# First chunk's q projection token tile by token tile, with weights in contiguous blocks of 128 channels

## The chip, the cores and the metric

One core of a Trainium2 chip runs the whole program. The metric is device time in microseconds (us) of one execution; lower is better. PE is TensorE's matmul side, PEld its weight loads, DVE is VectorE, ACT is ScalarE, SP is the engine whose queue issues nearly all DMAs. A hole is time on PE beyond the usual spacing between the starts of two matmuls. An evacuation copies a result out of PSUM, where this kernel's matmuls put it, into SBUF, where they read it.

A ratio is the mean time of one kernel's runs over that of the kernel before in the same rounds, so it is not quite the ratio of the medians quoted beside it.

## The reference, cut to what matters

Two layers, each an attention block with a residual and a gated feed-forward block with a residual, on 2,048 tokens of 1,024 channels in bf16:

```python
x = A_x                                              # [1, 2048, 1024]
x = x + _A_ref(_layernorm(x), A_wqkv, A_wo)          # q,k,v projections, 8 dilated keys per query, output projection
x = x + _B_ref(_layernorm(x), B_w1, B_w3, B_w2)      # silu(x w1) * (x w3), times w2
x = x + _A_ref(_layernorm(x), A_wqkv, A_wo)
x = x + _B_ref(_layernorm(x), B_w1, B_w3, B_w2)
```

Only the first thing that TensorE can do matters here: layernorm of the first 512 tokens ("chunk 0", four row tiles of 128 tokens) and their q projection with `A_wqkv[:, 0:1024]`.

## The kernel before

Tokens go in chunks of `CH = 512`. A chunk's normalized tokens are transposed into `xnT` (channel on the partition, token along the row). For q, k and v in turn, `q_part` multiplies 8 channel blocks of 128 by 8 contraction slices. The q, k, v projections of all four chunks come first, then attention (on DVE) and the feed-forward stages interleave.

The start of the kernel before normalizes all four row tiles, then projects:

```python
def ln_first(key):
    # ... stats on DVE for tiles 0..2, by two ACT accumulations for tile 3 ...
    warm(NWARM)                     # 13 dummy matmuls of 512 columns
    # stats, sqrt, apply and PE transposes of the 4 tiles, with 4 + 4 + 2 more dummy matmuls between them
    # evacuation of the transposes into xnT on ACT and DVE

def q_part(l, c, which, ws, then=()):
    first = (l, c) == (0, 0) and which < 2
    # ...
    for t0 in range(0, KT, SG):                         # SG = 2
        sgt = stg.tile([P, SG, CH], BF16, name="sgt")   # 3 staging buffers
        for t in range(t0, t0 + SG):
            ps = bank("ps")
            for kk in range(KT):
                nc.tensor.matmul(ps[:], lhsT=ws[kk // KH][:, kk % KH, t::KT], rhs=xnT[:, kk, :],
                                 start=(kk == 0), stop=(kk == KT - 1))
            # ...
            nc.scalar.copy(sgt[:, t - t0, :], ps[:])
            if first:                                   # attention's first q and k tile, directly
                nc.scalar.copy(now_T[:, t, HALO if which else 0:], ps[:, 0:TCH])
        nc.sync.dma_start(qkv_d[l][which][:, t0:t0 + SG, c * CH:(c + 1) * CH], sgt[:])
        # ... then[t0 // SG](): a later load
```

The weights are read with a step of 8 channels (`t::KT`), so that head channels land on the partitions that attention wants. Loads: x tiles 0, 1, 2 on SP and 3 on ACT's queue, then the q weights in four pieces of 512 KB, the k weights, x chunk 1. The loads of x chunk 2, both v weight tiles and x chunk 3 are issued one by one behind the four stores of q (`then`).

The order of work in the program is fixed when it is built, from a small cost model in the kernel (`now`, `x_at`): it decides after which projection step an output projection (`o_tile`, PE) of an attention half is placed:

```python
while o_queue and (must or oT_at.get((o_queue[0][0], o_queue[0][1] // 2), 1e9) + 0.3 <= now["pe"]):
    o_tile()
```

## Time and profile before

| | kernel before |
|---|---|
| time, median (range) | 1619.57 us (1619.52 to 1619.87, 6 runs) |
| span of the profiled run | 1617.9 us |
| first q matmul | 12.20 us |
| end of q (64 matmuls, 0.216 us apart) | about 26.0 us |
| q weight pieces landed (the trace's DMA records) | 8.19, 9.53, 10.87, 12.23 us |
| attention's first multiply on DVE | 45.86 us |

The page of the kernel before, its part on the chain that ended last (followed back from the last instruction, at each step to what released it; shares of the span by engine, then by line):

```profile
PE 98%; DVE 1%; issue 1%; DMA 0%; ACT 0%; SPq 0%; DVEq 0%
PE acc L609 24%; PE pu L593 23%; PE pg L585 23%; PE ps L543 20%; PE po L501 7%; DVE tm L432 0%; DMA x_sb<-in_A_x_dram 0%; DVE tm L317 0%; DVE hT L597 0%; DVE st L246 0%; DVE At L416 0%; DVE xn L259 0%; ACT xnT L277 0%; DVE xnT L277 0%; PE pT L269 0%
```

TensorE is the chain. The list of waits of PE alone, in the whole span (engine, line, what it waited for, us in total, times, longest):

```profile
PE pw L173 <- DVE hT L166: 1.2, 1, 1.2
PE pT L269 <- DVE xn L259: 0.6, 1, 0.6
PE ps L543 <- DVE xnT L277: 0.3, 1, 0.3
```

All three lie in the first 12.2 us. From the first q matmul on, PE starts a 512-column matmul every 0.216 us, to the last few. So the time is a prologue, a fixed amount of PE work, and a tail.

The timeline of the kernel before, a few lines of the prologue (start us, duration us, engine, line, operation, tiles, count, and in brackets the idle time before and who ended it):

```profile
1.19 5.51 PE L173 MATMUL pw<-hT 128*128 128x512 bf16 x13 [1.19 <-DVE hT L166]
...
6.61 0.62 PE L269 MATMUL pT<-ident,xn 128*128 128x128 bf16 x8
...
11.36 1.09 DVE L277 COPY xnT<-pT 128x1024 bf16<-128x1024 bf16 x3 [0.16 <-PE pT L269]
12.17 19.85 PEld L543 LDWEIGHTS <-wqkv 128*128 128x128 bf16 x93 [0.47 <-issue]
12.20 20.05 PE L543 MATMUL ps<-xnT,wqkv 128*128 128x512 bf16 x90 [0.33 <-DVE xnT L277]
```

The 13 dummy matmuls (5.51 us) start 0.427 us apart, where 512-column matmuls later start 0.216 us apart; that is what "half clock" means below. (The trace's granted clock says 1.00 there too; the spacing is what shows it.) The transposes of tile 0 follow at 6.61, and useful work starts at 12.20, released by an evacuation into `xnT` on DVE. Further on one hand-over is tight. The timeline of the kernel before again, at the output projection of the second attention half (`oT` is attention's result, L501 reads it):

```profile
160.19 0.29 DVE L319 TENSOR_TENSOR oT<-tm 128x256 bf16<-128x256 bf16 x1
160.51 3.34 PEld L501 LDWEIGHTS <-oT 128*128 128x128 bf16 x16
```

The first weight load of the projection starts at 160.51. The eight pieces of `oT` are read one after the other, 0.216 us apart, so the last one is needed at about 160.51 + 7 x 0.216 = 162.0; it is finished at 160.19 + 0.29 = 160.48.

### The profile page before, as it was taken

The numbers are of one execution on the slowest core, as the hardware profiler recorded it, in microseconds if no ns is written. First come the engines' busy times: TensorE is split into PE (matmuls) and PEld (weight loads), VectorE is DVE, ScalarE is ACT, GpSimd is POOL, SyncE is SP. The second block draws the span as 40 slices with busy tenths as digits, with TensorE's granted clock in tenths as the row PEclk, the third lists the DMA queues.
The fourth block names the chain that finished last, engine by engine and source line by source line (L and its number), as shares of the span: only waits on it lengthen the run. The fifth ranks groups of instructions, "written<-read, shape, count | busy, mean of one in ns | idle before, by whom it ended". The sixth has DMA issues, their size and how long they took to land.

```text
span 1617.9 us, 18887 instructions
## 1 busy us (share of the span) xinstructions
PE 1604.7 (99%) x7342; PEld 802.1 (50%) x7491; DVE 1176.1 (73%) x1962; ACT 358.8 (22%) x558; POOL 1.9 (0%) x12
## 2 busy tenths in 40 slices
PE   9999999999999999999999999999999999999999
PEld 5666544444445544455444554445544444444444
DVE  5999898989899899998998449983499832222222
ACT  5333311212112230222302123021230212011110
POOL 0000000000000000000000000000000000000000
PEclk9999999999999999999999999999999999999999
DMA  9465755466537664578553676538674265436430
GB/s 317 133 180 168 244 182 161 137 190 196 169 106 235 222 194 131 171 208 249 158 182 120 213 241 170 187 101 255 213 223 157 92 195 170 143 108 217 157 130 27
DMA packets 335322, 285.28 MB, mean 176 GB/s; under 512 B 69632, under 2 KB 317824, under 8 KB 335104
## 3 DMA queue, kind: packets, MB, share of 16 engines
q1 hardware_dynamic: 334944, 283.67, 57.7%
q8 instruction: 58, 0.95, 0.2%
q10 hardware_dynamic: 288, 0.39, 0.1%
q14 instruction: 32, 0.26, 0.0%
HBM read 238.94 MB, written 29.36 MB: 166 GB/s over the span
## 4 chain that ended last, share of the span: by engine, by line
PE 98%; DVE 1%; issue 1%; DMA 0%; ACT 0%; SPq 0%; DVEq 0%
PE acc L609 24%; PE pu L593 23%; PE pg L585 23%; PE ps L543 20%; PE po L501 7%; DVE tm L432 0%; DMA x_sb<-in_A_x_dram 0%; DVE tm L317 0%; DVE hT L597 0%; DVE st L246 0%; DVE At L416 0%; DVE xn L259 0%; ACT xnT L277 0%; DVE xnT L277 0%; PE pT L269 0%
## 5 line engine op out<-in xcount | busy, mean ns | idle before, releaser
L593 PE MATMUL pu<-xnT,w3t 128*128 128x512 bf16 x1760 | 420.8, 379 | 2.1
L585 PE MATMUL pg<-xnT,w1t 128*128 128x512 bf16 x1751 | 419.2, 379 | 1.8
L609 PE MATMUL acc<-w2t,hT 128*128 128x512 bf16 (+1 forms) x1769 | 387.7, 378 | 1.8
L543 PE MATMUL ps<-xnT,wqkv 128*128 128x512 bf16 x1506 | 331.3, 379 | 1.9 <-DVE xnT L277 0.3
L589 ACT ACTIVATE sg<-pg 128x512 bf16<-128x512 f32 x224 | 133.6, 597 | 767.5 <-PE pg L585 709.4
L597 DVE TENSOR_TENSOR hT<-sg,pu 128x512 bf16<-128x512 bf16 x224 | 152.8, 682 | 185.3 <-PE pu L593 173.7
L609 PEld LDWEIGHTS <-hT 128*128 128x128 bf16 x1804 | 176.6, 98 | 210.5
L593 PEld LDWEIGHTS <-w3t 128*128 128x128 bf16 x1792 | 175.4, 98 | 211.4
L585 PEld LDWEIGHTS <-w1t 128*128 128x128 bf16 x1792 | 175.3, 98 | 211.4
L543 PEld LDWEIGHTS <-wqkv 128*128 128x128 bf16 x1536 | 220.3, 143 | 111.9 <-issue 0.5
L372 DVE TENSOR_TENSOR pr<-qT,kT 128x2048 bf16<-128x2048 bf16 x128 | 156.4, 1222 | 88.5 <-DMA kT<-qkv_d 86.4
L547 ACT CAST sgt<-ps 128x512 bf16<-128x512 f32 x192 | 111.9, 585 | 243.1 <-PE ps L543 218.0
L619 DVE TENSOR_TENSOR x_sb<-x_sb,acc 128x512 bf16<-128x512 bf16 x129 | 87.4, 677 | 107.5 <-PE acc L609 102.8
L432 DVE TENSOR_TENSOR tm<-At,vT 128x2048 bf16<-128x2048 bf16 x128 | 156.3, 1221 | 2.4
L317 DVE TENSOR_TENSOR tm<-tm 128x1024 bf16<-128x1024 bf16 (+1 forms) x256 | 134.7, 552 | 0.4
L317 DVE TENSOR_TENSOR pr<-pr 128x1024 bf16<-128x1024 bf16 (+1 forms) x256 | 134.5, 553 | 0.5
L501 PE MATMUL po<-wo,oT 128*128 128x512 bf16 x501 | 115.2, 379 | 0.6
L192 DVE BATCH_NORM_STATS2 st<-x_sb 128x6 f32<-128x512 bf16 x120 | 75.9, 672 | 8.8 <-DMA x_sb<-in_A_x_dram 8.8
L501 PEld LDWEIGHTS <-oT 128*128 128x128 bf16 x512 | 50.1, 98 | 60.0
L506 DVE TENSOR_TENSOR x_sb<-x_sb,po 128x512 bf16<-128x512 bf16 x64 | 43.4, 685 | 20.9 <-PE po L501 20.6
L589 ACT ACT_TABLE_LOAD x31 | 39.8, 1283 | 50.5 <-PE pg L585 46.2
L319 DVE TENSOR_TENSOR psm<-pr 128x256 bf16<-128x256 bf16 x128 | 36.7, 287 | 0.5
(88 smaller groups left out, 377.1 us busy)
## 6 DMA issues: line engine op xcount, KB each, us to landing
w1t<-in_B_w_dram SPq DMA_DIRECT2D x56, 1024.0 KB, 5.6
w3t<-in_B_w_dram SPq DMA_DIRECT2D x56, 1024.0 KB, 8.0
w2t<-in_B_w_dram SPq DMA_DIRECT2D x48, 1024.0 KB, 5.3
wqkv<-in_A_wqkv_dram SPq DMA_DIRECT2D x28, 1024.0 KB, 6.9
qkv_d<-sgt SPq DMA_DIRECT2D x96, 256.0 KB, 3.1
w2t<-in_B_w_dram SPq DMA_DIRECT2D x16, 512.0 KB, 5.1
qT<-qkv_d SPq DMA_DIRECT2D x15, 512.0 KB, 9.1
kT<-qkv_d SPq DMA_DIRECT2D x14, 544.0 KB, 9.2
```

The lines of the kernel that those rows point to most:

```text
L317: nc.vector.tensor_tensor(b[:, 0:m, :], b[:, 0:m, :], b[:, m:2 * m, :], op=ALU.add)
L372: V.tensor_tensor(pr[:], qT[:], kT[:, :, k0:k0 + TCH], op=ALU.mult)
L432: V.tensor_tensor(tm[:], At[:], win, op=ALU.mult)
L501: nc.tensor.matmul(ps[:], lhsT=oT[:, t, j * P:(j + 1) * P], rhs=wo[:, t, hh * 512:(hh + 1) * 512], start=(t == 0), stop=(t == KT - 1))
L543: nc.tensor.matmul(ps[:], lhsT=ws[kk // KH][:, kk % KH, t::KT], rhs=xnT[:, kk, :], start=(kk == 0), stop=(kk == KT - 1))
L547: nc.scalar.copy(sgt[:, t - t0, :], ps[:])
L585: nc.tensor.matmul(pg[:], lhsT=w1t[:, kk, fi * P:(fi + 1) * P], rhs=xnT[:, kk, :], start=(kk == 0), stop=(kk == KT - 1))
L589: nc.scalar.activation(sg[:], pg[:], ACTF.Silu)
L593: nc.tensor.matmul(pu[:], lhsT=w3t[:, kk, fi * P:(fi + 1) * P], rhs=xnT[:, kk, :], start=(kk == 0), stop=(kk == KT - 1))
L597: nc.vector.tensor_tensor(hT[:, f - f0, :], sg[:], pu[:], op=ALU.mult)
L609: nc.tensor.matmul(acc[:], lhsT=hT[:, f - f0, j * P:(j + 1) * P], rhs=w2ts[(f - f0) // 8][:, (f - f0) % 8, q0:q0 + step], start=(f == f0), ...
L619: nc.vector.tensor_tensor(xs, xs, acc[:], op=ALU.add)
```

## The change

The intent is to start useful matmuls right after the first row tile's norm (near 7 us) instead of after the fourth's (12.2 us). With 128 tokens in hand a matmul has 128 columns, so the weights should load fast; they are now read in contiguous blocks of 128 channels, and the store to DRAM puts channels back where attention expects them. Attention's first q tile is then loaded from DRAM rather than copied from PSUM. Weights come in slices of 256 KB, interleaved with the x tiles. The dummy matmuls between transposes are gone.

```diff
-    def ln_first(key):                       # all four norms, then q_part(0, 0, 0)
+    def first_q(ws, loads, then):
+        q_rows = qkv_d[0][0][:].rearrange("i t s -> (i t) s").rearrange("(b p) s -> p b s", p=P)
+        load_tile(0, 0, 512, nc.sync)
+        load_tile(0, 512, D, nc.scalar)
+        load_tile(1, 0, D, nc.sync)
+        loads(0, 2)                          # weight slices 0, 1
+        load_tile(2, 0, D, nc.sync)
+        loads(2, 4)
+        load_tile(3, 0, D, nc.sync)
+        loads(4, 8)                          # then k weights, x chunk 1
         ...
+        def product(out, kk, b, tok, start, stop):
+            nc.tensor.matmul(out, lhsT=ws[kk // KH][:, kk % KH, b * P:(b + 1) * P], rhs=xnT[:, kk, tok], ...)
         ...                                  # norm, transpose, evacuation of tile 0
+        for kk in range(6):                  # tile 0, 128 columns, one weight slice after the other
+            step0(kk)
+        stats(2, 0)
+        xn = apply(1)
+        pTs = transpose(xn)
+        for h in range(2):
+            evacuate(1, h, pTs, nc.scalar.copy)
+        for kk in range(6, KT):
+            step0(kk)
+        stats(2, 1)
+        deviation(2)
         ...
+        stats(3, 0)
+        xn = apply(2)
+        stats(3, 1)
+        deviation(3)
+        for b in range(3):                   # tile 1, 128 columns; transposes of tiles 2 and 3 in between
+            block1(b)
         ...
+        tok = slice(2 * P, CH)               # tiles 2 and 3 together, 256 columns
+        for i, acc in enumerate(accumulators(2, 2 * P)):
             ...
+            nc.scalar.copy(hT[:, 2 * i:2 * i + 2, tok], acc[:])
+            nc.sync.dma_start(q_rows[:, 2 * i:2 * i + 2, 0:CH], hT[:, 2 * i:2 * i + 2, :])
+            then[i]()                        # x chunk 2, v weights, x chunk 3
@@ q_part (now k of chunk 0 first)
+            if first and t0 == SG:
+                load_part(qT, 0, 0, 0, False)    # attention's first q tile, from DRAM
@@ planner
-    now = dict(pe=12.5, dve=12.5, act=12.5, table=None)
-    x_at = [12.5, 22.0, 27.0, 36.0]
+    now = dict(pe=22.0, dve=15.0, act=22.0, table=None)
+    x_at = [12.5, 20.0, 25.0, 34.0]
```

The planner's start values are changed along with the rest.

## The prediction

> **What bounds it now.** TensorE. The page gives PE 99% busy and 98% of the chain of work that ended last. Reading PE's instructions in order of time, the matmuls of 512 columns start 0.216 us apart from 12.2 us to 1614.5 us, with no hole above 20 ns that isn't a missing record. So the time is about 12.2 us of prologue, some 7,424 matmuls at 0.216, and a 3 us tail. Only the stretch up to the end of the first q projection (64 matmuls, 12.2 to about 26.0 us) changes.
>
> **The prologue now.** Timeline: 13 cold warm-up matmuls 0.427 us apart until 6.6 us; first transposes at 6.6; last norm evacuation near 12.4; first q matmul at 12.2. The DMA issues of the trace land the q weights at 8.2, 9.5, 10.9 and 12.2 us; the windows show 356 to 397 GB/s from 5 us on. So norm and weights finish together: starting tile by tile helps only as far as weights are there.
>
> **Cost of the new order.** 128-column products: the transposes in the timeline (8 in 0.62 us, the last end modelled 0.22 us long) start 56 ns apart, each with its own weight load. The Trainium skill, "TensorE: Matmul & The Clock Gate", Back-to-back issue gap, gives 55.6 ns alone, but about 81 ns sustained for load-and-matmul streams; I follow the trace. Two tiles are 2 x 64 x 56 ns = 7.2 us, the 256-column rest 64 x 0.109 = 7.0 us, transposes of tiles 1 to 3 1.35 us: 15.5 us against 13.8 + 0.
>
> Bytes are unchanged (1 MB x, 2 MB weights before k), so I estimate w5 at about 10.7 us and w7 at about 12.1. Tile 0 therefore crawls at weight speed (0.67 us a slice, 0.45 us of work) and ends at 12.6. Then ACT is the brake: evacuation of tile 1 in two copies (0.58 us each, between the 0.37 and 1.0 us seen for 256 and 1024 elements), the square roots of tiles 2 and 3 behind it in its order. I expect holes of about 0.5 us before tile 1 and 0.5 us before tile 3's transposes. q then ends at 12.6 + 3.6 + 0.9 + 7.0 + 1.0 = about 25.0, against 26.0. DMA a bit earlier would give 24.
>
> **Downstream.** All of that 1 to 2 us lies on PE's chain, since PE never waits later. Against it: the loads of x chunks 2 and 3 hang on the later q stores (first store near 20.5 us against 16.5), so attention on VectorE starts no earlier (45.9 us now). The second attention half ends at 160.5 us and its output projection starts at 160.7: an earlier PE may wait there and give back up to 1 us, unless the planner moves that tile one step later.
>
> **Predicted: 1618.4 us, range 1616.6 to 1619.9.** Faster by over 2%: 0.01; within 2%: 0.98; slower: 0.01.
>
> **Right if:** first q matmul at about 7.5 us; 128-column matmuls 56 ns apart; tile 0's steps released by weight DMAs; q's last matmul at 24 to 25.5 us; k, v and all later work spaced 0.216, shifted by a constant.
>
> **Wrong if:** q ends by 22 to 23 (weights land earlier than I estimate: about 1616); 128-column pairs take 80 ns (q ends 3 us later: about 1621); the clock gate drops to half because the PE is only about 65% busy from 7 to 12 us and the filler matmuls are gone (same page, HAM: an idle window of about 3.4 us throttles; here 107 ns spacing would show it, costing 1 to 2 us); or a wait of the first output projections for attention returns the gain.

## More of the kernel before

Staging buffers (`sgt`) hold results until a DMA has stored them.

Runs of one submission share a chip and share the runs of the kernel before.

## The result, and the profile after

| | before | after |
|---|---|---|
| time, median (range), 6 runs each | 1619.57 us (1619.52 to 1619.87) | 1618.28 us (1617.55 to 1619.09) |
| span of the profiled run | 1617.9 us | 1616.3 us |
| first q matmul | 12.20 us | 7.35 us |
| end of q (start of k) | about 26.0 us | 24.64 us |
| last q weights landed | 12.23 us | 12.22 us |
| PE's last matmul starts | 1614.50 us | 1613.09 us |
| attention's first multiply | 45.86 us | 47.74 us |

The ratio is 0.9992, with an interval of 0.9979 to 1.0005. In all rounds, though, the slowest of the changed kernel's 11 timed runs (1619.22 us) is faster than the fastest of the kernel before's (1619.40 us): a gain of about 1 us is there. Also new is the scatter: a range of 1.5 us against 0.35.

The page after, chain that ended last:

```profile
PE 99%; DMA 0%; SPq 0%; DVE 0%; ACT 0%; issue 0%
PE acc L658 24%; PE pu L642 24%; PE pg L634 24%; PE ps L591 20%; PE po L552 7%; PE pq L283 1%; DMA wqkv<-in_A_wqkv_dram 0%; SPq L683 0%; SPq L241 0%; DVE xn L266 0%; ACT xnT L280 0%; PE pT L275 0%; DVE st L255 0%; ACT sd L259 0%; DVE x_sb L668 0%
```

The q weights (`DMA wqkv<-in_A_wqkv_dram`) now stand on the chain, in place of the norm. PE's instructions after, in order of time:

```profile
6.28 0.72 PE L275 MATMUL pT<-ident,xn 128*128 128x128 bf16 x8
7.35 2.19 PE L283 MATMUL pq<-xnT,wqkv 128*128 128x128 bf16 x32 [0.35 <-ACT xnT L280]
10.25 1.30 PE L283 MATMUL pq<-xnT,wqkv 128*128 128x128 bf16 x16 [0.70 <-DVE st L255]
11.38 0.61 PE L275 MATMUL pT<-ident,xn 128*128 128x128 bf16 x8
11.83 2.40 PE L283 MATMUL pq<-xnT,wqkv 128*128 128x128 bf16 x40
14.06 0.61 PE L275 MATMUL pT<-ident,xn 128*128 128x128 bf16 x8
14.51 1.06 PE L283 MATMUL pq<-xnT,wqkv 128*128 128x128 bf16 x16
15.86 0.62 PE L275 MATMUL pT<-ident,xn 128*128 128x128 bf16 x8 [0.29 <-DVE xn L266]
16.32 8.49 PE L283 MATMUL pq<-xnT,wqkv 128*128 128x128 bf16 x88
24.64 1.67 PE L591 MATMUL ps<-xnT,wqkv 128*128 128x512 bf16 x7
```

Read single, the 128-column products start 56 ns apart and the 256-column ones 109 ns apart. The first 24 run without a break, the weight slices 0 to 2 having landed; slices 3, 4 and 5 each give a burst of 8 that had to wait for its slice. The trace's DMA records land the eight slices at 5.98, 6.63, 7.99, 8.88, 10.20, 10.88, 11.54 and 12.22 us; the hole that ends at 10.25 is thus slice 4. (The view puts it down to `DVE st`, whose instruction happened to end at 10.25 too. PE reads nothing of it; the weight load just before, at 10.24, waited 0.87 us for `DMA wqkv`, and in the run `wlate` below the hole itself is put down to the DMA.) Behind slice 7 there is one hole, 0.45 us before 15.86, where tile 3's norm comes late. The chain that ended last, in order of time, ties both together:

```profile
5.11 5.77 DMA wqkv<-in_A_wqkv_dram
10.88 0.05 issue
10.93 0.62 PE pq L283 x8
...
15.86 0.62 PE pT L275 x8
```

The last landing on it is slice 5's (10.88). Behind its 8 products PE transposes tile 1, ACT evacuates it (from 11.81), and only then comes tile 2's square root in ACT's order (12.88), and tile 3's norm after that (14.73 to 15.81). Slices 6 and 7 aren't on this chain, but slice 7 is a near tie: PE's work from slice 5's first product (10.93) to slice 7's (12.28) takes 1.35 us, the landings of the two are 1.34 us apart. So a distance counted from slice 7, as in the table below, serves as well as one counted from slice 5.

Behind q, PE has no hole over 20 ns in this run. From k's first matmul to PE's last one it takes 1588.45 us, as before (about 1588.5, with q's end worked out as 12.20 + 64 x 0.216). That distance will be used below: what it exceeds 1588.45 by is PE time lost behind q.

The slack at the output projection of the second attention half is now gone. The timeline after:

```profile
159.11 1.39 PEld L552 LDWEIGHTS <-oT 128*128 128x128 bf16 x7
...
160.38 0.29 DVE L371 TENSOR_TENSOR oT<-tm 128x256 bf16<-128x256 bf16 x1
160.73 1.71 PEld L552 LDWEIGHTS <-oT 128*128 128x128 bf16 x9 [0.23 <-DVE oT L371]
```

PE came 1.4 us earlier, attention 0.2 us later, which uses up the 1.5 us. The eighth weight load of the tile now waits for the last piece of `oT`, 0.23 us, which the matmuls in flight just cover.

Why attention didn't come earlier too: the timeline after, among k's results:

```profile
39.76 0.59 ACT L595 CAST sgt<-ps 128x512 bf16<-128x512 f32 x1 [3.48 <-DMA qkv_d<-sgt]
...
40.51 0.31 ACT L194 ACTIVATE sd<-mv,epst 128x2 f32<-128x2 f32 x1
...
40.85 0.17 DVE L201 RECIPROCAL rstd<-sd 128x2 f32<-128x2 f32 x1 [2.29 <-ACT sd L194]
```

ACT stands 3.48 us for a staging buffer (`sgt`) whose store sits in the SP queue behind later loads and DMA transposes. A norm's square root is next in ACT's order, DVE waits 2.29 us for it, and attention is next in DVE's order.

### The profile page after: what moved, and what is told of

It reads as the page before. It is cut to its first block, busy times and chain, and to the rows that moved or that the text cites. A ratio compares the mean times of both kernels' runs of the same rounds, so it can differ in the third digit from the quotient of the medians. Undisturbed runs are those within 1.5% of the kernel's fastest.

```text
span 1616.3 us, 19263 instructions
## 1 busy us (share of the span) xinstructions
PE 1610.7 (100%) x7609; PEld 805.3 (50%) x7609; DVE 1176.6 (73%) x1965; ACT 353.6 (22%) x547; POOL 1.9 (0%) x12
## 4 chain that ended last, share of the span: by engine, by line
PE 99%; DMA 0%; SPq 0%; DVE 0%; ACT 0%; issue 0%
PE acc L658 24%; PE pu L642 24%; PE pg L634 24%; PE ps L591 20%; PE po L552 7%; PE pq L283 1%; DMA wqkv<-in_A_wqkv_dram 0%; SPq L683 0%; SPq L241 0%; DVE xn L266 0%; ACT xnT L280 0%; PE pT L275 0%; DVE st L255 0%; ACT sd L259 0%; DVE x_sb L668 0%
## 5 line engine op out<-in xcount | busy, mean ns | idle before, releaser
L591 PE MATMUL ps<-xnT,wqkv 128*128 128x512 bf16 x1472 | 319.2, 379 | 0.0
L591 PEld LDWEIGHTS <-wqkv 128*128 128x128 bf16 x1472 | 211.1, 143 | 106.7
L595 ACT CAST sgt<-ps 128x512 bf16<-128x512 f32 x184 | 106.7, 585 | 230.7 <-PE ps L591 211.9
L446 DVE STREAM_TRANSPOSE psmT<-psm 128x2048 bf16<-128x2048 bf16 x16 | 36.9, 2306 | 0.2
```

## The experiments

All kernels gave correct results. Where a run's edit is said to be on top of another, it has that one's edit too. The table gives what the profiled run of each shows. "Slice 7" is the landing of the last q weights, "q end" the start of k's first matmul, "lost" the PE time lost behind q as defined above, "attention" the start of its first multiply. Every time is in us; the last column is the kernel before.

| run | slice 7 | q end | q end minus slice 7 | lost | attention | median (range) | before |
|---|---|---|---|---|---|---|---|
| after (result) | 12.22 | 24.64 | 12.42 | 0.00 | 47.74 | 1618.28 (1617.55 to 1619.09) | 1619.57 |
| again | 11.82 | 24.24 | 12.42 | 0.89 | 48.30 | 1618.72 (1618.48 to 1619.22) | 1619.61 |
| wlate | 12.56 | 24.98 | 12.42 | 0.87 | 48.99 | 1619.73 (1619.00 to 1620.16) | 1619.61 |
| norms | 12.49 | 24.45 | 11.96 | 1.09 | 48.71 | 1618.49 (1618.02 to 1619.02) | 1619.61 |
| strided | 12.10 | 24.78 | 12.68 | 1.02 | 48.96 | 1618.58 (1618.53 to 1619.29) | 1619.61 |
| loads | 11.88 | 24.30 | 12.42 | 0.01 | 45.82 | 1618.11 (1617.42 to 1618.55) | 1619.64 |
| dual | 12.18 | 23.41 | 11.23 | 0.45 | 47.02 | 1617.86 (1617.34 to 1618.19) | 1619.64 |
| dual_loads | 12.35 | 23.37 | 11.02 | 0.04 | 46.57 | 1616.69 (1616.59 to 1616.89) | 1619.64 |
| later_tile | 12.51 | 24.92 | 12.41 | 0.81 | 48.92 | 1619.21 (1618.54 to 1619.48) | 1619.44 |
| norms_loads | 12.66 | 24.62 | 11.96 | 0.00 | 46.10 | 1617.38 (1617.13 to 1618.11) | 1619.44 |
| nofill | 11.96 | 25.09 | 13.13 | 0.00 | 46.37 | 1618.70 (1618.58 to 1618.93) | 1619.44 |
| before_loads | 12.08 | about 25.7 | | 2.3 | 51.01 | 1621.47 (1621.25 to 1621.58) | 1619.44 |

### The changed kernel again

No edit.

> The changed kernel once more, unedited. Theory (the weight slices' landings set when tile 0 ends, the rest of the q projection is PE work, and everything behind it only shifts): last q matmul hands over to k at 24.6 us within 0.5, no hole on PE after it, time 1.0 to 1.7 us under the kernel before. Rival (the gain is noise between placements of runs): interval around the ratio spans 1 by more than 0.0005 on both sides. A spread of the runs of about 1 us, against 0.3 us for the kernel before, would say that the weight landings' jitter now stands on the chain.

The median is 0.9 us under the kernel before, less than the 1.0 expected; the ratio's interval (0.9983 to 1.0008) again spans 1, by more than 0.0005 on both sides. By the criterion set beforehand the rival (noise) thus stands after this run; against it speaks that none of the timed runs of the two kernels overlap, as said above. Its profiled run is not like the first. q ended 0.4 us earlier, in step with slice 7, but PE lost 0.89 us behind q. The weight loads' timeline says where:

```profile
158.71 1.18 PEld L552 LDWEIGHTS <-oT 128*128 128x128 bf16 x6
160.65 0.10 PEld L552 LDWEIGHTS <-oT 128*128 128x128 bf16 x1 [0.76 <-DVE oT L371]
161.30 1.63 PEld L552 LDWEIGHTS <-oT 128*128 128x128 bf16 x9 [0.56 <-DVE oT L371]
```

The output projection of the second attention half waited for attention. "No hole behind q", as I had expected, was wrong.

### Weight slices 4 to 7 later

```diff
         load_tile(3, 0, D, nc.sync)
+        nc.sync.dma_start(x_sb[:, 4, :], xin[:, 4, :])   # loaded again later with chunk 1
         loads(4, 8)
```

> One more 256 KB load (a row tile that is loaded again later) goes ahead of weight slices 4 to 7, so these land about 0.67 us later (slice 7 at 12.9 instead of 12.2 us); nothing else is touched. Theory (weight landings bound the first tile): the end of q moves by 0.6 to 0.7 us, to about 25.3, and the time rises by 0.6 us over the unedited changed kernel of the same rounds. Rival (the norm chain on ACT and DVE is what PE waits for): the hole before tile 3's transposes shrinks to nothing and takes up the delay, end of q moves by under 0.25 us.

Slice 7 landed 0.74 us later than in `again`, and q ended 0.74 us later: the distance from the one to the other stays 12.42 us. (Kernels without the extra load landed slice 7 as late as 12.66 us too, so the delay against one run could be chance; but within this run slice 4 lands 2.01 us behind slice 3, against 1.35 in `again`.) All five runs with this q stage and warm-up (`after`, `again`, `wlate`, `loads`, `later_tile`) have a distance of 12.41 to 12.43 us, with slice 7 anywhere from 11.82 to 12.56. PE's timeline shows the longer hole with its true cause:

```profile
10.58 1.30 PE L284 MATMUL pq<-xnT,wqkv 128*128 128x128 bf16 x16 [1.25 <-DMA wqkv<-in_A_wqkv_dram]
```

With equal losses behind q (0.87 and 0.89), the profiled spans differ by 0.8 us, the medians by 1.0. The landing of the weights sets the end of q, one for one; the rival (the norm chain would have absorbed the delay) falls, since tile 2's square root itself stands behind slice 5 in PE's and ACT's order. The extra load also delays what is queued behind it (the k weights landed at 15.26 instead of 14.54 us, long before PE reads them).

### Norms of tiles 2 and 3 earlier

```diff
         stats(2, 0)
         xn = apply(1)
+        stats(2, 1)
+        deviation(2)
+        stats(3, 0)
+        stats(3, 1)
+        deviation(3)
         pTs = transpose(xn)
         ...
-        stats(2, 1) ; deviation(2)        # were here, behind tile 1's evacuation
         ...
-        stats(3, 0) ; xn = apply(2) ; stats(3, 1) ; deviation(3)
+        xn = apply(2) ; xn3 = apply(3)
```

> The statistics and square roots of tiles 2 and 3 move ahead of tile 1's evacuation in ACT's and DVE's order, so both normalized tiles are there by about 13.5 us. Theory: only the one hole of 0.45 us before tile 3's transposes goes; q ends at about 24.2 and the time falls by 0.4 us. Rival (the norm chain is the main brake of the whole stage): q ends over 1 us earlier. If q ends earlier and the time doesn't fall, the first output projections wait for attention (the third of them had its last operand with no time to spare).

The hole of 0.45 us went: q ends 11.96 us behind slice 7 instead of 12.42. But the profiled run lost 1.09 us behind q, and the median is only 0.2 us under `again`, within the scatter. By itself this run doesn't show a gain in time.

### Strided weights again

```diff
-lhsT=ws[kk // KH][:, kk % KH, b * P:(b + 1) * P]
+lhsT=ws[kk // KH][:, kk % KH, b::KT]
-nc.sync.dma_start(q_rows[:, 2 * i:2 * i + 2, 0:CH], hT[:, 2 * i:2 * i + 2, :])
+nc.sync.dma_start(qkv_d[0][0][:, 2 * i:2 * i + 2, 0:CH], hT[:, 2 * i:2 * i + 2, :])
```

> The contiguous blocks of 128 channels undone: weights read with a step of 8 channels as in the kernel before, output stored in the old layout; same tile-by-tile order. If the block layout matters because a strided weight load can't hide behind 128 columns: spacing of 128-column products rises from 56 ns to between 85 and 145 ns, that of the 256-column ones stays 109 or rises to up to 145, q ends 3 to 9 us later and the time rises by as much, above the kernel before. If the weight load hides or only its record is longer: spacing stays 56 ns and nothing changes.

This undoes half of the change. The instructions of the product's line, with strided weights (durations in ns, minimum, median, maximum, then first and last start):

```profile
L283 PEld LDWEIGHTS <-wqkv x192: 142/146/166, 6.8 to 24.6; 128*128 128x128 bf16 x192
```

and in the changed kernel:

```profile
L283 PEld LDWEIGHTS <-wqkv x192: 95/98/99, 6.8 to 24.4; 128*128 128x128 bf16 x192
```

A weight load's record is half as long again, yet the 128-column products start 61 to 62 ns apart instead of 56, and the 256-column ones 109 as before. Both of my cases missed: the load hides nearly whole. The end of q, counted from slice 7, moved by 0.26 us only (12.68): behind slice 5 the products took 0.56 us longer in all, but the hole before tile 3's transposes shrank from 0.45 to 0.12 us and took up more than half of that. The median can't resolve it. So the block layout is worth about a quarter of a microsecond here; the start tile by tile is the rest. Without that hole (as in `norms`) it may be worth up to the 0.56 us, an estimate from these two traces; no run shows it.

### x and v weight loads early

```diff
             load_x(1)
+            load_x(2) ; load_weight() ; load_weight() ; load_x(3)
-    first_q(w_tiles[0:2], load_wq, (lambda: load_x(2), load_weight, load_weight, lambda: load_x(3)))
+    first_q(w_tiles[0:2], load_wq, (lambda: None,) * 4)
```

> The loads of x chunks 2 and 3 and of the two v weight tiles are issued right behind x chunk 1 instead of behind the q stores. Theory: no time is gained (PE has no hole behind q), median within 0.4 us of the changed kernel, but attention's first multiply starts earlier than 47.7 us, by 2 us or more, and the third output projection finds its operand over 1 us early. If the scatter of the changed kernel's runs came from that tight operand, the spread falls too; if it comes from the weight landings, it stays near 1 us.

Attention starts at 45.8 us, nothing is lost behind q, and the median is the lowest of the kernels with an unchanged q stage. The gain over the changed kernel (0.2 to 0.6 us, across submissions) is small, as it must be where a wait of 0 to 1 us goes. The last piece of `oT` was finished at 158.8 us, 0.2 us before the projection's first matmul, and it is needed 1.5 us after that: over 1 us early, as expected. The scatter stayed at 1.1 us: by the expectation's rule that part belongs to the weights' landing (more on this at the end).

### Tile 1 as filler while weights land

```diff
-        for kk in range(6):
-            step0(kk)
+        for kk in range(3):
+            step(acc0, 0, kk)                # tile 0, slices 0 to 2
         stats(2, 0)
         xn = apply(1)
         pTs = transpose(xn)
+        evacuate(1, 0, pTs, nc.scalar.copy)
+        stats(2, 1)
+        evacuate(1, 1, pTs, nc.vector.tensor_copy)
+        # deviation(2), stats and deviation of tile 3, apply of both, on DVE and ACT
+        step(acc0, 0, 3)
+        for kk in range(4):
+            step(acc1, 1, kk)                # tile 1, slices 0 to 3
+        for kk in range(4, KT):
+            step(acc0, 0, kk)
+        # tile 1 slices 4, 5; transposes of tiles 2, 3; tile 1 slices 6, 7; then 256 columns as before
```

> Tile 1 is transposed after three weight slices instead of six and its products fill the time in which tile 0 waits for weights (accumulators of both tiles open at once); norms of tiles 2 and 3 ahead, two tile evacuations shared by ACT and DVE. Theory: with that work the weight wait is hidden, q ends at about 23.3 us (PE work bound: 7.35 + 15.5 us = 22.9). But attention then comes too late for the third output projection: PE waits about 1 us near 158 us and the time falls by only 0.2 to 0.5 us against the changed kernel. Rival (no such margin): the time falls by the full 1.3 us.

q ended at 23.41 us, as expected, and no longer 12.42 us behind slice 7 but 11.23. The loss behind q was 0.45 us in the profiled run. The median is 0.4 us under that of the first six runs of the changed kernel and 0.9 us under `again`, not the 1.2 us that q gained (counted from slice 7).

### Both

The edits of `dual` and `loads` together.

> Both edits: tile 1 as filler, and the x and v weight loads issued early so that attention starts earlier. Theory: q ends at about 23.3 us, no PE hole at the third output projection, the time is 1.2 us under the changed kernel and 2.5 us under the kernel before. Rival (attention's start has nothing to do with it): same time as with the filler alone.

1616.69 us: 2.95 us under the kernel before (ratio 0.9982, interval 0.9968 to 0.9995, the only one of the faster ones wholly under 1) and about 1.6 to 2.0 us under the changed kernel. Nothing to speak of is lost behind q, and the scatter is down to 0.3 us. The weights' landing no longer stands on the chain of the profiled run: up to k it begins with `DMA x_sb<-in_A_x_dram` and has no `wqkv` transfer on it. PE's order of time:

```profile
6.49 0.72 PE L275 MATMUL pT<-ident,xn 128*128 128x128 bf16 x8 [0.79 <-DVE xn L266]
7.56 1.50 PE L283 MATMUL pq<-xnT,wqkv 128*128 128x128 bf16 x24 [0.35 <-ACT xnT L280]
9.06 0.62 PE L275 MATMUL pT<-ident,xn 128*128 128x128 bf16 x8
9.52 5.24 PE L283 MATMUL pq<-xnT,wqkv 128*128 128x128 bf16 x88
14.60 1.06 PE L275 MATMUL pT<-ident,xn 128*128 128x128 bf16 x16
15.49 8.04 PE L283 MATMUL pq<-xnT,wqkv 128*128 128x128 bf16 x80
23.37 0.81 PE L583 MATMUL ps<-xnT,wqkv 128*128 128x512 bf16 x2
```

From 9.52 us on, 88 products run almost without a break where the changed kernel had bursts. This is the best version. It has no slack left either: at the tight projection one weight load waits 0.35 us for attention, which the matmuls in flight cover but for 0.04 us.

### Early loads in the kernel before

```diff
     load_x(1)
+    load_x(2) ; load_weight() ; load_weight() ; load_x(3)
-    then = (lambda: load_x(2), load_weight, load_weight, lambda: load_x(3))
+    then = ()
```

> The kernel before, with the one edit that its x and v weight loads are issued at the start, as in the run with early loads. Theory (PE never waits after q in the kernel before, so earlier loads can't help it): time within 0.3 us of the kernel before. Rival (the early loads are the gain by themselves and tile-by-tile q adds little): 1 us or more faster.

Neither: it is 2.0 us slower. Here q is still staged in the three `sgt` buffers, and its stores now queue behind 4 MB of loads. The timelines of ACT and of the weight loads:

```profile
32.55 0.59 ACT L547 CAST sgt<-ps 128x512 bf16<-128x512 f32 x1 [8.29 <-DMA qkv_d<-sgt]
...
163.45 0.10 PEld L501 LDWEIGHTS <-oT 128*128 128x128 bf16 x1 [2.12 <-DVE oT L319]
```

ACT stands 8.29 us for a staging buffer, a norm's square root stands behind it, attention starts at 51.0 us instead of 45.9, and at the same output projection as ever PE pays 2.1 us and a little more. The early loads are no gain by themselves. That they help the changed kernel fits its q going to DRAM out of `hT`, which holds all of q at once, so that q's copies on ACT wait for no store there; no run changes the staging alone, so this cause is read from the traces and not tested.

### The tight output projection one step later

```diff
-... + 0.3 <= now["pe"]
+... + (3.75 if o_queue[0] == (0, 2) else 0.3) <= now["pe"]
```

> The changed kernel with the third output projection placed one step (two q channel blocks, 3.45 us) later in PE's order, nothing else. Theory (that projection waits 0 to 1.1 us for attention, by how late attention starts): no PE loss behind q, as with early loads, so a median near 1618.1 and 0.2 to 0.7 us under the unedited changed kernel; the profiled distance from k's first matmul to PE's last one is 1588.5 us instead of up to 1589.5. Rival (the loss sits elsewhere): same loss, only moved.

My expectation failed. The projection moved to 163.1 us and waited no more, but 0.81 us were lost further on. PE's timeline, at the first matmul of the feed-forward stage:

```profile
191.49 1.89 PE L634 MATMUL pg<-xnT,w1t 128*128 128x512 bf16 x8 [0.65 <-DMA xnT<-xn]
```

The feed-forward needs that projection's result, normalized and transposed. Moved later, the projection makes its next reader late. The rival ("same loss, only moved") was right: this placement has no free slack either. What does cure the loss is an earlier attention, as `loads` shows.

### Early norms on top of early loads

The edits of `norms` and `loads` together.

> Early norms of tiles 2 and 3, with the early loads that take the wait for attention away. Theory: q ends 11.96 us after slice 7 lands (12.42 without the early norms) and now the 0.45 us arrive in the time: 1617.6 to 1617.7, against 1618.1 with early loads alone. Rival (the early norms are worth nothing): same as early loads alone.

q ended 11.96 us behind slice 7, nothing was lost behind q, and the median is 2.06 us under the kernel before of its rounds, where `loads` was 1.53 under it: 0.5 us for the 0.46 us hole. That is what the early norms should pay without the wait for attention, though the slices landed late in the profiled run (12.66). The traces show it; the times only fit it, since the runs of the two kernels overlap (1.09 to 2.22 us under the median of the kernel before for `loads`, 1.33 to 2.31 here).

### No warm-up matmuls

```diff
-    NWARM = 13
+    NWARM = 0
```

on top of `loads`.

> Early loads, and no warm-up matmuls at all (13 before). If weight landings bound tile 0 and the clock recovers during its crawl: the first transposes and products are 107 ns apart, later ones 56 ns, q ends at most 0.5 us later against slice 7's landing. If the clock gate stays at half because the crawl is too thin to open it: 107 ns spacing holds past slice 7, q ends 3 us or more later and the time is over 1620.5 us.

PE's timeline:

```profile
6.04 1.04 PE L275 MATMUL pT<-ident,xn 128*128 128x128 bf16 x8 [6.04 <-DVE xn L266]
7.33 4.66 PE L283 MATMUL pq<-xnT,wqkv 128*128 128x128 bf16 x48 [0.25 <-ACT xnT L280]
```

The products start 107 ns apart until 11.2 us and 56 ns apart from there. q ended 13.13 us behind slice 7 (12.42 with the dummies): 0.71 us, a little over the 0.5 I had allowed, and the time agrees (0.74 us under the kernel before, `loads` 1.53). Cold, a slice's 8 products take 0.85 us and slices land 0.67 us apart, so PE falls 0.7 us behind the landings and doesn't catch up; the slow products cost no more than that because they also fill the 0.8 us for which PE waits for slices 4 and 5 in `loads`. The crawl of tile 0 does open the clock gate (the prediction's word for the switch from the slow spacing to the full one).

## Why the prediction was right

The predicted 1618.4 us (1616.6 to 1619.9) met 1618.28.

- **What the number alone tests.** Little: the range also held the kernel before's own 1619.57. The marks on the way are the test, and in the time two deviations pull against each other: q ended 0.4 us earlier than predicted (0.8 in `again`), and up to 1.1 us was given back later. That the profiled run of the result gave nothing back is luck of that run: attention finished its last piece of `oT` at 160.67 us there, and at 161.25 to 161.97 in the five others with late x loads and the q stage tile after tile.
- **What bounds it.** Right. PE is the chain, and the end of q carries over: 26.0 to 24.64 us in q's end, 1614.50 to 1613.09 in PE's last matmul.
- **Landings of the weights.** Predicted slice 5 at about 10.7 and slice 7 at about 12.1; measured 10.88 and 12.22. `wlate` shows that this time passes to the end of q one for one. ("Tile 0's steps released by weight DMAs" held for slices 3 to 5, and slice 7 by a near tie.)
- **Cost of a 128-column product.** 56 ns, as the transposes of the trace before had said. The Trainium skill, "TensorE: Matmul & The Clock Gate", section Back-to-back issue gap, gives both about 56 ns for a single product and about 81 ns as the sustained figure for load-and-matmul streams. The stream here has a fresh weight load for each product and runs at 56. (The prediction's 55.6 stands on the same page in another section.)
- **The sum to q's end.** 12.6 + 3.6 + 0.9 + 7.0 + 1.0 = 25.1, given as about 25.0; 24.64 measured. The over-sized term is the last one, the holes. The hole before tile 3's transposes was there (0.45 us, predicted 0.5), and it is ACT's order that made it (`norms`). The one expected before tile 1 wasn't: tile 0's slices 6 and 7 covered the evacuation.
- **Attention no earlier.** It came 1.9 us later than before. I had blamed the x loads for hanging on q's stores; the trace shows a staging buffer's store in the SP queue and a square root behind it on ACT, and no wait of DVE for x between 30 and 48 us. The loads have a part in it all the same: issued early, in `loads`, they let that store go at 34.38 instead of 37.16 us and attention start at 45.82.
- **"May give back up to 1 us".** It does: nothing in the profiled run of the result, 0.87 to 1.09 us in the profiled runs of `again`, `wlate`, `norms` and `strided`, and in `later_tile` elsewhere. Of the kernels without early loads, "shifted by a constant" held only in the first. I had put the slack there at 0.2 us, from attention's end to the projection's start; counted to the read of the last piece it was 1.5 us, which is why the gain of 1.4 us could come through at all.
- **The clock gate.** No product behind the warm-up ran at half clock, though PE waited between bursts; the longest stretch without a new product was 1.5 us (`wlate`, start to start). The skill's page (same title, section "Why this matters for your kernels") advises no idle gaps over about 3 us; no gap here was that long, so the runs fit the advice and don't test it.

What stays open: where the scatter of the weights' landing comes from (slice 7 at 11.82 to 12.66 us across runs). That the remaining 1.1 us of scatter in `loads` is this landing is inferred from `dual_loads` and `nofill`, where the chain has no weight landing on it and the scatter is 0.30 and 0.35 us; of `norms_loads`, which has one, it is 0.98. Also open is why attention ended later in the other runs than in the result's, in `again` though q ended earlier.

## What to carry to other kernels

Where one engine streams without holes, a start that is earlier by 1.4 us is worth 1.4 us at most, and only if each later hand-over has that much slack: look up the tightest one in the trace before (here 1.5 us at 160.5 us, counted to the read of the last piece) before counting on more. Starting on the first tile helps until the next thing that arrives late, here the weights; independent work on the second tile is the filler for that wait. And when an edit that should be harmless costs time (early loads in the kernel before), look for a staging buffer whose store queues behind the new traffic.

## What the Trainium skill lacked or had wrong

- "TensorE: Matmul & The Clock Gate", Back-to-back issue gap: the sustained roofline figures for load-and-matmul streams, about 81 ns at 128 columns and about 131 ns at 512, are not what these streams do: 56 ns and 216 ns between starts, each with its own weight load. The page's formula for the isolated gap fits (109 ns at 256 columns too).
- The same page, the section on fast weight load, allows a column step and says nothing of its cost (the page "SBUF — State Buffer" speaks of a penalty for accesses that leave a 16-byte line, without a figure for weight loads): with a step of 8 elements a weight load's record took 146 ns instead of 98, but the products started only 5 to 6 ns further apart at 128 columns, and no further at 256.
- The same page, Part 1 (the HAM clock gate), puts the change to full clock around 4 us into sustained matmuls, give or take 0.5 us: here the first full-clock spacing began 3.2 to 5.9 us after the first dummy matmul (at 4.4 to 7.1 us, the dummy at 1.19), by the run. The band is too narrow; a note further down in the same Part, that one kernel measured 6, 11 or 14 cold matmuls, is nearer.
- "DMA: Bandwidth & Descriptors", Specifications, gives an HBM limit per core of about 358 GB/s without a condition: the window from 7 to 12.2 us of the kernel before moved 394 GB/s, nearly all of it loads. Further down the same page says that each core gets about 358 when both cores of the domain stream, which one core alone doesn't contradict; the row lacks that condition.
- No page that I read says how a build-time order of work keeps or loses slack at later hand-overs; here a slack of 1.5 us, once used up, cost up to 1.1 us.
